# Attention in front of two MoE layers on one core: AV's last 64 keys in half-width products, the mixed step with rotated keys, 1/sum spread on GpSimd and turned a slot later

## The chip, the core and the metric

The kernel runs on one NeuronCore of a Trainium2 chip. The metric is the device time of one launch in microseconds, the median of several executions. TensorE (PE) multiplies, VectorE (DVE), ScalarE (ACT) and GpSimd (POOL) do the element-wise work, SyncE (SP) issues the DMAs. Each engine takes its instructions in the order in which they stand in its own queue.

## What is computed

An attention with a bias that a small network makes from positions, and behind it two MoE-like dense layers on its output, all in float32:

```python
scores = scale * q @ k.T + bias            # bias[h] = relu(log-distance ratio @ w1 + b1) @ w2
attn = exp(scores - max(scores))
attn = attn / (sum(attn) + 1e-9)
x = (attn @ v) as (B*S, H*D)               # B, H, S, D = 4, 8, 576, 64
h = x @ w_in                               # 512 -> 2048 -> 512
x = (h * clip(h + 3, 0, 6) / 6) @ w_out
y = (sigmoid(x @ w_gate) * (x @ w_val)) @ w_out2   # 512 -> 1536 -> 512
```

## The kernel before

The program has four stages. The **bias stage** (lines 508 to 593) makes the position bias in 36 groups G of 16 rows: DVE, and ACT for one tile of every second group, make four hidden tiles (L570, L572), PE multiplies them (L578), ACT evacuates each group in two pieces (L557), and SP writes it to DRAM (`nbias`, L560), from where `load_bias` fetches it. Then comes **attention** (slots of two steps, `slot_of_two`), then the first dense layer (`out1`, `project`), then the second (`gate_val`, `out2`).

Attention treats 16 units n, each a pair of heads of one batch. A unit has nine steps s of 128 query rows: steps 0 to 7 are 128 rows of one head (head s % 2, rows 128 * (s // 2)), and step 8, the mixed step, holds the last 64 rows of both heads, head 0 in partitions 0 to 63 and head 1 in 64 to 127. A slot holds two steps, so a unit is 4.5 slots, and even and odd units lie differently in them.

For a step, `scores` (L342) makes q times k in two halves of 288 keys, with q and k each as a high and a low float32r part; DVE adds the bias and takes the row extreme (L346); ACT takes the exponential with the row sum (`expo`, L362). The probabilities are turned on PE, 128 keys by 128 rows at a time (`trans`, L400), and copied to `ptm`, DVE and ACT in turns. Of 576 keys, 512 go so in four pieces (head 0 the first 512, head 1 the last 512), and the remaining 64 keys of both heads are turned together in one piece into `ptr` (`trans_rem`, L415). In the mixed step, `trans` turns 64 rows of each head apart (L408, eight turns of 64 by 128, one group per head), and `trans_rem` two pieces more (L418, L419); `Pm`, the mixed step's probabilities, has 64 zero columns in front for that.

`av` multiplies: for g = 0 to 3 two products of 64 output columns each, one per head, which fill the two halves of the array (L432), and for the remaining 64 keys one product of 128 columns, whose weights are v of both heads in block form (L435). `AV` sets in which slot each goes. A unit's AV is done in two halves `a` of 288 query rows, each in one slot with g = 0 to 2 and the next one with g = 3 and the remaining keys; behind it `av_out` multiplies by `inv` (L444).

`inv` is 1/sum with queries along the free dimension. `invert` adds 1e-9 to the row sums and takes the reciprocal on DVE (L368, L369), and ACT spreads each sum over 64 or 128 columns of `spread` (L373), one copy after the unit's step 5 and two after step 8. `turn_inv` turns `spread` on PE (L379, three and two turns) into a tile of the ring `tr`, and ACT and DVE copy that to `inv`. The ring `tr` has three tiles in PSUM, for all turns. `invert` is called a slot behind its step, `turn_inv` two slots behind, below scores and AV.

`prep` splits the next unit's q and k into high and low parts, q's high part on ACT (L310), the rest on GpSimd (L314, L318). `load_qk` fetches q and k for that into `early`; for unit 1 it is called in the bias stage at G = 20. Weights for the dense layers are taken in by `load.whole()` at every sixth slot, with work on ACT, DVE and GpSimd (L175 to L193).

The Tile framework lays each engine's queue out by its own estimate of when operands are ready, so the order in a queue is near the order of the code, but not the same.

Of the kernel before, what the change touches and what calls it, by code (L numbers as in the profile page):

```python
# [18 lines left out]
P = 128  # L19
# [77 lines left out]
def block_kernel(ctx: ExitStack, tc: tile.TileContext, q, k, v, mlp, w_in, w_out, w_gate, w_val, w_out2, dist_d,  # L97
# [12 lines left out]
    one = keep.tile([P, 1], F32, name="one")  # L110
    slots = [keep.tile([P, 2, 512], F32R, name=f"slot{i}") for i in range(NPRE)]
# [166 lines left out]
    Pm = [apool.tile([P, S + 64], F32, name=f"pm{i}") for i in range(2)]  # L278
# [18 lines left out]
    def load_bias(p, c):  # L297
        n = min(P, S - P * c)
        rows_of = nbias[c][15 : 15 + n * (8 * RK - 1)].rearrange("(i q) -> i q", i=n)
        for h in range(2):  # L300
            o = bias_t[c][:, h] if c < 4 else bias_m[64 * h : 64 * h + 64]
            nc.sync.dma_start(o, rows_of[:, RK * (2 * p + h) : RK * (2 * p + h) + S])
# [29 lines left out]

    def scores(t):
# [4 lines left out]
        for a in range(2):  # L338
            mm = [(h, c, r) for h, c in todo for r in range(2)]
            for i, (h, c, r) in enumerate(mm):  # L340
                q0 = (0, S + P)[h] + P * c if c < 4 else (512, S)[h]
                last_s[0] = nc.tensor.matmul(ps[:, a, 0:HS], Q[:, q0 : q0 + P], K[:, r, h, HS * a : HS * a + HS],  # L342
                                 start=(i == 0), stop=(i == len(mm) - 1))
# [7 lines left out]
    def probs(t):  # L351
        n, s = seq[t]
        if s < 8:
            c, h = divmod(s, 2)
            if h == 0:
                pts[n, c] = a2.tile([P, 2, S], F32, name="p", bufs=3)
            return pts[n, c][:, h]
        return Pm[n % 2][:, 64:]
# [6 lines left out]
    def invert(n, c0, c1):  # L365

        r = sums[n % 3][:, 2 * c0 : min(2 * c1, NSTEP)]
        nc.vector.tensor_scalar(out=r, in0=r, scalar1=1e-9, scalar2=None, op0=ALU.add)  # L368
        nc.vector.reciprocal(r, r)  # L369
        for s0, s1, w in ((0, 6, 64),) if c1 == 3 else ((6, 8, 64), (8, 9, P)):  # L370
            o = spread[:, 64 * s0 : 64 * s0 + (s1 - s0) * w].rearrange("p (s w) -> p s w", w=w)
            i = sums[n % 3][:, s0:s1].unsqueeze(2).to_broadcast(o.shape)
            nc.scalar.copy(o, i)  # L373
# [20 lines left out]
    def trans(t):  # L394
# [7 lines left out]
        else:  # L402
            pm = Pm[n % 2]
            for h in range(2):
                ps = pp.tile([P, 4, P], F32, name="tr", bufs=3)
                r = slice(64 * h, 64 * h + 64)
                for kc in range(4):
                    nc.tensor.transpose(ps[:, kc, 0:64], pm[r, 64 + 64 * h + P * kc : 64 + 64 * h + P * kc + P],  # L408
                                        ident[r, r])
                evac("AV"[h], ptm[:, h, :, 512:S], ps[:, :, 0:64])  # L410

    def trans_rem(n, c):
# [3 lines left out]
        if c == 3:  # L416
            pm = Pm[n % 2]
            nc.tensor.transpose(ps[:, 1], pm[:, 0:P], ident)  # L418
            nc.tensor.transpose(ps[0:64, 2], pm[:, S : S + 64], ident)  # L419
            evac("A", ptr[0:64, 512:S], ps[0:64, 2, 0:64])  # L420
            evac("V", ptr[64:P, 512:S], ps[64:P, 1, 64:P])
        evac("A", ptr[:, P * c : P * c + P], ps[:, 0])

    def av(n, a, g):
# [9 lines left out]
        else:  # L434
            nc.tensor.matmul(ps[:, 0:HS], vt[:, 8:10].rearrange("p a d -> p (a d)"), ptr[:, cols], start=False, stop=True)  # L435
# [27 lines left out]
    def slot_of_two(i):  # L463

        for t in steps(i):
# [17 lines left out]
        for t in steps(i - 2):  # L483
            n, s = seq[t]
            if s in (5, 8):
                turn_inv(n, s // 6 * 3, s // 6 * 2 + 3)
# [19 lines left out]
    with ExitStack():  # L506
# [11 lines left out]
        nc.vector.memset(one, 1.0)  # L518
        nc.scalar.activation(low[0][:, 0:1], one, AF.Relu)
# [7 lines left out]
        for i in range(2):  # L527
            nc.gpsimd.memset(Pm[i][:, 0:64], 0.0)
# [35 lines left out]
        for G in range(NG):  # L564
# [24 lines left out]
            if G == 20:  # L589
# [336 lines left out]
```

## Time and profile before

| | before |
|---|---|
| median of 3 runs | 1162.75 us (1162.29 to 1164.39) |
| the profiled execution | 1162.39 us |
| its span on the core | 1160.6 us |
| bias stage, attention, first dense layer, second | 0 to 60, 60 to 345, 345 to 743, 743 to 1160 us |

Windows of the trace give the busy time of each engine in a stretch, which shows what a stage has to spare. The waits say what PE stood still for. The timeline of PE gives the start of each run of equal matmuls; since PE works in order, the distance between two starts is what the run between them took, switches of the array included. A float32 product shows as two records per instruction there (`x4` is two instructions), a float32r product or a turn as one. Starts are rounded to 0.01 us.

### The profile page before, as it was taken

To read this page: it belongs to the slowest core of one execution; us is meant where nothing else is said; L and a number is where in the kernel's file an instruction comes from. 1 tells how busy PE (TensorE), PEld (TensorE's weight loads), DVE (VectorE), ACT (ScalarE), POOL (GpSimd) and SP (SyncE) were. 2 spreads that over 40 slices of the span, in tenths; PEclk is the share of its full clock that TensorE was granted. 3 is DMA by queue.
4 is the path that set the end of the run, shared out by engine and by line. 5 is a ranking of instruction groups with operands and counts; after the bars stand their busy time and mean duration, and the time that the engine had idled before them with its cause. 6 is when DMAs were issued, how large, how long until landed. Compare 5 with 4: busy or idle time off the path is not lost.

```text
span 1160.6 us, 19146 instructions
## 1 busy us (share of the span) xinstructions
PE 1139.1 (98%) x6862; PEld 1012.1 (87%) x6862; DVE 776.1 (67%) x1495; ACT 587.6 (51%) x1296; POOL 424.3 (37%) x342
## 2 busy tenths in 40 slices
PE   8799999999999999999999999999999999999998
PEld 3277777777779999999999999999899898998997
DVE  8977887878868887456377685585367655644443
ACT  7888877877855455454455445342333232221221
POOL 0235545545306343232346545261333223311211
PEclk9999999999999999999999999999999999999999
DMA  6853536354213565349566759976878848757532
GB/s 203 276 170 92 178 96 189 94 148 139 79 55 110 196 218 195 118 171 325 183 228 245 253 189 357 394 260 254 314 254 309 305 165 303 282 186 255 190 109 73
DMA packets 83183, 236.82 MB, mean 204 GB/s; under 512 B 9616, under 2 KB 12304, under 8 KB 83088
## 3 DMA queue, kind: packets, MB, share of 16 engines
q1 hardware_dynamic: 83088, 235.60, 58.5%
q8 instruction: 54, 0.88, 0.3%
q14 instruction: 41, 0.34, 0.1%
HBM read 154.15 MB, written 81.41 MB: 203 GB/s over the span
## 4 chain that ended last, share of the span: by engine, by line
PE 84%; DVE 7%; ACT 2%; issue 2%; POOL 1%; DMA 1%; SPq 0%; DVEq 0%; POOLq 0%; ACTq 0%
PE o L673 17%; PE h L807 10%; PE o L807 10%; PE s L342 6%; PE o L862 6%; PE h L862 5%; PE h L612 5%; PE h L610 5%; PE h L611 5%; PE av L432 5%; PE tr L400 4%; PE av L435 1%; DVE z L186 1%; DVE u L346 1%; DVE x L572 1%
## 5 line engine op out<-in xcount | busy, mean ns | idle before, releaser
L673 PE MATMUL o<-gh,slot 128*128 128x384 f32 x768 | 195.1, 334 | 1.8 <-DVE take L392 1.8
L673 PEld LDWEIGHTS o<-gh,slot 128*128 128x128 f32 x768 | 138.5, 188 | 2.4 <-DVE take L392 2.1
L673 PE MATMUL o<-gl,slot 128*128 128x384 f32 x384 | 128.5, 335 | 0.5 <-DVE gl L659 0.5
L362 ACT ACTIVATE p<-u,stat 128x576 f32<-128x576 f32 x128 | 98.7, 774 | 29.2 <-DVE stat L346 28.6
L342 PE MATMUL s<-k,q 128*128 128x288 f32 x640 | 111.1, 309 | 0.3 <-DVE stat L346 0.3
L346 DVE CUSTOM_DVE_ANT_0 u<-s,bias 128x576 f32<-128x576 f32 x128 | 93.5, 752 | 23.9 <-PE s L342 22.8
L843 POOL TENSOR_TENSOR gp<-s,gp 128x384 fp32r<-128x384 f32 x36 | 39.4, 1107 | 177.0 <-ACT gp L842 92.7
L658 ACT CAST gh<-g 128x384 fp32r<-128x384 f32 x94 | 48.2, 513 | 97.7 <-DVE g L617 97.4
L617 DVE SCALAR_TENSOR_TENSOR g<-g,h 128x384 f32<-128x384 f32 x94 | 51.5, 548 | 68.4 <-ACT g L616 68.4
L659 DVE TENSOR_TENSOR gl<-g,gh 128x384 fp32r<-128x384 f32 x94 | 63.2, 672 | 48.5 <-ACT gh L658 47.4
L193 POOL TENSOR_TENSOR hl<-corners,hl 128x512 fp32r<-128x512 f32 x42 | 57.2, 1365 | 93.9 <-ACT hl L192 77.6
L342 PEld LDWEIGHTS s<-k,q 128*128 128x128 f32 x640 | 88.8, 189 | 2.1 <-DVE stat L346 1.0
L616 ACT ACTIVATE g<-h,half 128x384 f32<-128x384 f32 x94 | 54.3, 578 | 52.0 <-PE h L612 51.5
L807 PE MATMUL o<-x,slot 128*128 128x384 f32 x432 | 78.4, 336 | 1.4 <-DVE sum L787 1.4
L432 PE MATMUL av<-ptm,vn 128*64 128x288 f32 x512 | 77.5, 419 | 0.7 <-DVE x L444 0.7
L807 PE MATMUL h<-x,slot 128*128 128x384 f32 x432 | 77.8, 335 | 0.0
L807 PEld LDWEIGHTS o<-x,slot 128*128 128x128 f32 x432 | 75.1, 188 | 2.0 <-DVE sum L787 1.7
L807 PEld LDWEIGHTS h<-x,slot 128*128 128x128 f32 x432 | 75.2, 188 | 0.7
L400 PE MATMUL tr<-ident,p 128*128 128x128 f32 x512 | 72.2, 275 | 2.3 <-ACT inv L390 1.5
L673 PEld LDWEIGHTS o<-gl,slot 128*128 128x128 f32 x384 | 72.1, 188 | 1.2 <-DVE gl L659 1.2
L843 POOL TENSOR_TENSOR x<-s,x 128x384 fp32r<-128x384 f32 x36 | 40.3, 1128 | 84.2 <-ACT x L842 50.2
L314 POOL TENSOR_TENSOR k<-early,one 128x576 fp32r<-128x576 f32 x30 | 35.4, 1202 | 95.1 <-PE s L342 52.9
(157 smaller groups left out, 2734.1 us busy)
## 6 DMA issues: line engine op xcount, KB each, us to landing
w<-hl SPq DMA_DIRECT2D x67, 512.0 KB, 3.4
slot<-w SPq DMA_DIRECT2D x67, 512.0 KB, 5.9
raw<-in_part_dram SPq DMA_DIRECT2D x50, 512.0 KB, 4.0
x<-xc SPq DMA_DIRECT2D x56, 384.0 KB, 6.2
sum<-sum SPq DMA_DIRECT2D x72, 256.0 KB, 3.4
early<-xc SPq DMA_DIRECT2D x28, 384.0 KB, 6.3
nbias<-ptm SPq DMA_DIRECT2D x36, 295.5 KB, 2.7
early<-in_part_dram SPq DMA_DIRECT2D x32, 288.0 KB, 4.3
```

What stands on the lines that cost most here:

```text
L342: last_s[0] = nc.tensor.matmul(ps[:, a, 0:HS], Q[:, q0 : q0 + P], K[:, r, h, HS * a : HS * a + HS], start=(i == 0), stop=(i == len(mm) - 1))
L346: last_u[0] = nc.vector.tensor_tensor_reduce(out=halves(u), in0=ps[:, :, 0:HS], in1=halves(bt), op0=ALU.add, op1=ALU.min, scale=-0.125, sc ...
L362: nc.scalar.activation(probs(t), us.pop(t), AF.Exp, bias=low[n % 2][:, s : s + 1], scale=-1.0, accum_out=sums[n % 3][:, s : s + 1])
L400: nc.tensor.transpose(ps[:, kc], pts[n, c][:, h, 64 * h + P * kc : 64 * h + P * kc + P], ident)
L432: nc.tensor.matmul(ps[64 * h : 64 * h + 64, 0:HS], vt[:, 4 * h + g], ptm[:, h, g, cols], start=(g == 0), stop=False)
L610: nc.tensor.matmul(ps[:, 0:TW], wh, XH[:, c], start=(c == 0), stop=False)
L611: nc.tensor.matmul(ps[:, 0:TW], wl, XH[:, c], start=False, stop=False)
L659: last_g[0] = nc.vector.tensor_tensor(out=gl, in0=g, in1=gh.bitcast(F32), op=ALU.subtract)
L673: nc.tensor.matmul(os[c][:, 0:TW], sl[:, r, P * c : P * c + P], x, start=(first and r == 0 and x is gh), stop=(last and x is gl))
L807: nc.tensor.matmul(ps[b], sl[:, r, o : o + P], x[:, c, s], start=(k < 4 and i == 0), stop=(i == len(mm) - 1), skip_group_check=True)
L843: nc.gpsimd.tensor_tensor(out=G[:, i, 1], in0=s, in1=G[:, i, 0].bitcast(F32), op=ALU.subtract)
L862: nc.tensor.matmul(os[i], x[:, P * i : P * i + P], slots[(base + 14 + e) % NALL][:, r], start=first, stop=last)
```

## The change

- AV's remaining 64 keys are two products of 64 output columns, one per head, instead of one of 128 (`av`).
- In the mixed step, head 1's keys are taken in rotated order: 64 to 575, then 0 to 63. So both heads' first 512 columns of `Pm` are turned together, 4 turns of 128 by 128 and one copy (DVE in even units, ACT in odd), and the remaining 64 columns of both in one turn. The zero columns of `Pm` go. For the order, `scores` makes head 1's second half of that step in pieces of 224 and 64 columns, and `load_bias` fetches its bias rows in two pieces.
- `invert` adds 1e-9 as a tensor (`tiny`), and spreads on GpSimd instead of ACT.
- `turn_inv` is called three slots behind its step, above the slot's scores.
- `load_qk(1)` is called at G = 33.

```diff
@@ load_bias
-            nc.sync.dma_start(o, rows_of[:, RK * (2 * p + h) : RK * (2 * p + h) + S])
+            i = rows_of[:, RK * (2 * p + h) : RK * (2 * p + h) + S]
+            if c == 4 and h == 1:
+                nc.sync.dma_start(o[:, 0:512], i[:, 64:S])
+                nc.sync.dma_start(o[:, 512:S], i[:, 0:64])
+            else:
+                nc.sync.dma_start(o, i)
@@ scores
+    def keys(s, h, a):
+
+        if s < 8 or h == 0:
+            return [(HS * a, 0, HS)]
+        return [(64, 0, HS)] if a == 0 else [(64 + HS, 0, HS - 64), (0, HS - 64, 64)]
...
-            mm = [(h, c, r) for h, c in todo for r in range(2)]
+            mm = [(h, c, r, part) for h, c in todo for r in range(2) for part in keys(s, h, a)]
@@ invert
-        nc.vector.tensor_scalar(out=r, in0=r, scalar1=1e-9, scalar2=None, op0=ALU.add)
+        nc.vector.tensor_tensor(out=r, in0=r, in1=tiny.to_broadcast(r.shape), op=ALU.add)
...
-            nc.scalar.copy(o, i)
+            nc.gpsimd.tensor_tensor(out=o, in0=i, in1=one.unsqueeze(2).to_broadcast(o.shape), op=ALU.mult)
@@ trans
-            pm = Pm[n % 2]
-            for h in range(2):
-                ps = pp.tile([P, 4, P], F32, name="tr", bufs=3)
-                r = slice(64 * h, 64 * h + 64)
-                for kc in range(4):
-                    nc.tensor.transpose(ps[:, kc, 0:64], pm[r, 64 + 64 * h + P * kc : 64 + 64 * h + P * kc + P],
-                                        ident[r, r])
-                evac("AV"[h], ptm[:, h, :, 512:S], ps[:, :, 0:64])
+            ps = pp.tile([P, 4, P], F32, name="tr", bufs=3)
+            for kc in range(4):
+                nc.tensor.transpose(ps[:, kc], Pm[n % 2][:, P * kc : P * kc + P], ident)
+            evac("VA"[n % 2], ptm[:, :, :, 512:S], ps.rearrange("p c (h q) -> p h c q", h=2))
@@ trans_rem
-            pm = Pm[n % 2]
-            nc.tensor.transpose(ps[:, 1], pm[:, 0:P], ident)
-            nc.tensor.transpose(ps[0:64, 2], pm[:, S : S + 64], ident)
-            evac("A", ptr[0:64, 512:S], ps[0:64, 2, 0:64])
-            evac("V", ptr[64:P, 512:S], ps[64:P, 1, 64:P])
+            nc.tensor.transpose(ps[0:64, 1], Pm[n % 2][:, 512:S], ident)
+            for h in range(2):
+                evac("AV"[h], ptr[64 * h : 64 * h + 64, 512:S], ps[0:64, 1, 64 * h : 64 * h + 64])
@@ av
-            nc.tensor.matmul(ps[:, 0:HS], vt[:, 8:10].rearrange("p a d -> p (a d)"), ptr[:, cols], start=False, stop=True)
+            for h in range(2):
+                nc.tensor.matmul(ps[64 * h : 64 * h + 64, 0:HS], vt[:, 8 + h], ptr[:, cols], start=False, stop=True)
@@ slot_of_two
+        for t in steps(i - 3):
+            n, s = seq[t]
+            if s in (5, 8):
+                turn_inv(n, s // 6 * 3, s // 6 * 2 + 3)
         for t in steps(i):
             scores(t)
...
-        for t in steps(i - 2):
-            n, s = seq[t]
-            if s in (5, 8):
-                turn_inv(n, s // 6 * 3, s // 6 * 2 + 3)
@@ the bias stage
-            if G == 20:
+            if G == 33:
                 load_qk(1)
```

How the queues stand now is shown at three places; the line numbers of the changed program are a few higher (L342 is L354 there, L379 is L391, L400 is L412, L415 is L423, L432 is L438).

On PE in unit 5, behind AV's first half (`s` are scores, `tr` turns, `pm` the mixed step's probabilities, `spread` the sums), before:

```order
L379 MATMUL tr<-ident,spread 128x128 x3
L400 MATMUL tr<-ident,p 128x128 x4
L408 MATMUL tr<-ident,pm_233 128x64 x4
L342 MATMUL s<-k_230,q_228 128x288 x4
L408 MATMUL tr<-ident,pm_233 128x64 x4
L342 MATMUL s<-k_230,q_228 128x288
L415 MATMUL tr<-ident,p 128x128
L418 MATMUL tr<-ident,pm_233 128x128
L419 MATMUL tr<-ident,pm_233 64x128
```

and now:

```order
L412 MATMUL tr<-ident,p 128x128 x4
L417 MATMUL tr<-ident,pm_234 128x128 x4
L423 MATMUL tr<-ident,p 128x128
L425 MATMUL tr<-ident,pm_234 64x128
L354 MATMUL s<-k_231,q_229 128x288 x4
L391 MATMUL tr<-ident,spread 128x128 x3
L354 MATMUL s<-k_231,q_229 128x288 x4
```

The half-height turns, which stood in two groups with scores between them (in the eight odd units; in the eight even ones all eight stand together), are four full ones, and the turns of `spread` stand inside the scores.

On PE and on GpSimd around unit 7's second `turn_inv`, PE before:

```order
L435 MATMUL av<-ptr,vn 128x288
L379 MATMUL tr<-ident,spread 128x128 x2
L400 MATMUL tr<-ident,p 128x128 x8
L342 MATMUL s<-k_230,q_228 128x288 x7
L415 MATMUL tr<-ident,p 128x128
L342 MATMUL s<-k_230,q_228 128x288
L432 MATMUL av<-ptm,vn 64x288 x6
```

PE now:

```order
L442 MATMUL av<-ptr,vn 64x288 x2
L412 MATMUL tr<-ident,p 128x128 x8
L423 MATMUL tr<-ident,p 128x128
L354 MATMUL s<-k_231,q_229 128x288 x8
L438 MATMUL av<-ptm,vn 64x288
L391 MATMUL tr<-ident,spread 128x128 x2
L438 MATMUL av<-ptm,vn 64x288 x5
```

and GpSimd now, where `q` and `k` are the next unit's `prep`:

```order
L385 TENSOR_TENSOR spread<-stat,one 128x384
L320 TENSOR_TENSOR k_232<-early,one 128x576
L324 TENSOR_TENSOR k_232<-early,k_232 128x576
L320 TENSOR_TENSOR k_232<-early,one 128x576
L324 TENSOR_TENSOR k_232<-early,k_232 128x576
L324 TENSOR_TENSOR q_230<-early,q_230 64x640
L324 TENSOR_TENSOR q_230<-early,q_230 64x576
L385 TENSOR_TENSOR spread<-stat,one 128x128 x2
```

The turns of `spread` moved behind the scores and into a run of AV products, which they part into one and five; this is so in units 3, 7 and 11. The spread of the second sums stands behind the whole `prep` on GpSimd.

On SP in the bias stage, from group 16 on (`early` of 64x1152 is half of k, `bias` the bias of 128 rows), before:

```order
L560 DMA nbias_80<-ptm 128x591 x4
L291 DMA early<-in_part_dram 64x1152 x2
L560 DMA nbias_80<-ptm 128x591 x4
L560 DMA nbias_81<-ptm 128x591 x2
L302 DMA bias_224<-nbias_79 128x576 x2
L560 DMA nbias_81<-ptm 128x591 x6
L560 DMA nbias_82<-ptm 128x591 x4
```

and now:

```order
L566 DMA nbias_81<-ptm 128x591 x5
L308 DMA bias_225<-nbias_80 128x576
L566 DMA nbias_81<-ptm 128x591 x3
L308 DMA bias_225<-nbias_80 128x576
L566 DMA nbias_82<-ptm 128x591 x2
L292 DMA early<-in_part_dram 64x1152
L566 DMA nbias_82<-ptm 128x591 x4
L292 DMA early<-in_part_dram 64x1152
L566 DMA nbias_82<-ptm 128x591 x2
L566 DMA nbias_83<-ptm 128x591 x4
```

Both halves of k stood behind the write of group 19; now one stands behind that of group 25 and one behind that of group 29.

## Rows read from the trace of the kernel before

**Rows 1.** Windows: length, busy us of PE, PEld, DVE, ACT, POOL, clock.

```profile
60.00:345.00 285.00, 281.71 (x2063) 215.52 (x2062) 222.69 (x574) 226.75 (x591) 128.83 (x98) 1.00 0.41 121
345.00:743.00 398.00, 395.55 (x2276) 393.97 (x2275) 269.37 (x426) 195.92 (x380) 167.91 (x132) 1.00 0.62 223
```

**Rows 2.** Waits of PE in attention: us in total, times, longest.

```profile
PE tr L400 <- ACT inv L390: 1.5, 3, 0.5
PE tr L400 <- DVE ptm L392: 0.7, 3, 0.2
```

**Rows 3.** Timeline of PE in unit 6: start us, us.

```profile
171.13 0.71 PE L432 MATMUL av<-ptm,vn 128*64 128x288 f32 x4
171.77 0.75 PE L435 MATMUL av<-ptr,vn 128*128 128x288 f32 x2
172.36 1.04 PE L400 MATMUL tr<-ident,p 128*128 128x128 f32 x8
173.23 0.27 PE L415 MATMUL tr<-ident,p 128*128 128x128 f32 x1
...
175.03 1.68 PE L432 MATMUL av<-ptm,vn 128*64 128x288 f32 x12
176.64 0.55 PE L379 MATMUL tr<-ident,spread 128*128 128x128 f32 x3
177.02 1.04 PE L400 MATMUL tr<-ident,p 128*128 128x128 f32 x8
...
179.67 0.75 PE L435 MATMUL av<-ptr,vn 128*128 128x288 f32 x2
180.36 0.47 PE L408 MATMUL tr<-ident,pm 64*128 64x64 f32 x8
180.76 0.33 PE L415 MATMUL tr<-ident,p 128*128 128x128 f32 x1
180.93 0.27 PE L418 MATMUL tr<-ident,pm 128*128 128x128 f32 x1
```

**Rows 4.** Timeline of PE in unit 5, the mixed step's turns.

```profile
160.65 0.60 PE L400 MATMUL tr<-ident,p 128*128 128x128 f32 x4
161.18 0.46 PE L408 MATMUL tr<-ident,pm 64*128 64x64 f32 x4
...
162.93 0.27 PE L415 MATMUL tr<-ident,p 128*128 128x128 f32 x1
```

**Rows 5.** Windows of DVE's line 572 in the bias stage: length, busy us.

```profile
45.00:50.45 5.45, 5.42 (x5) 1.00 0.98 315
50.45:54.40 3.95, 3.95 (x11) 1.00 0.50 192
```

**Rows 6.** Timeline of GpSimd in the bias stage.

```profile
43.34 3.88 POOL L314 TENSOR_TENSOR k<-early,one 128x576 fp32r<-128x576 f32 x2 [41.90 <-DMA early<-in_part_dram]
47.18 3.08 POOL L318 TENSOR_TENSOR k<-early,k 128x576 fp32r<-128x576 f32 x2
```

**Rows 7.** Timeline of ACT in the bias stage.

```profile
51.61 1.09 ACT L557 ACTIVATE ptm<-s,corr,early 128x112 f32<-128x112 f32 x2 [2.51 <-PE s L578]
```

**Rows 8.** Window of all engines in the bias stage, as in rows 1.

```profile
50.30:61.50 11.20, 10.61 (x90) 4.81 (x90) 9.22 (x23) 9.16 (x18) 1.55 (x1) 1.00 0.53 201
```

**Rows 9.** SP's queue in the bias stage: start of the first, time to the last.

```profile
37.42 2.20 SPq L291 DMA_DIRECT2D early<-in_part_dram  x2
...
46.58 15.27 SPq L560 DMA_DIRECT2D nbias<-ptm  x10
```

**Rows 10.** Timeline of GpSimd in unit 7's `prep`.

```profile
190.56 2.25 POOL L314 TENSOR_TENSOR k<-early,one 128x576 fp32r<-128x576 f32 x2 [8.18 <-PE s L342]
...
199.42 1.42 POOL L318 TENSOR_TENSOR q<-early,q 64x576 fp32r<-64x576 f32 x1 [2.21 <-ACT q L310]
```

**Rows 11.** Timeline of PE at the same place.

```profile
201.81 1.68 PE L432 MATMUL av<-ptm,vn 128*64 128x288 f32 x12 [0.23 <-DVE x L444]
```

**Rows 12.** One line of DVE: times, ns min/median/max, first and last start.

```profile
L659 DVE TENSOR_TENSOR gl<-g,gh x94: 545/559/1644, 358.0 to 737.9; 128x384 fp32r<-128x384 f32 x94
```

More of the change, by code (lines that the diff above doesn't have):

```diff
@@ L110, in block_kernel @@
     one = keep.tile([P, 1], F32, name="one")
+    tiny = keep.tile([P, 1], F32, name="tiny")
     slots = [keep.tile([P, 2, 512], F32R, name=f"slot{i}") for i in range(NPRE)]
@@ L277, in block_kernel @@
     Ks = [apool.tile([P, 2, 2, S], F32R, name=f"k{i}") for i in range(2)]
-    Pm = [apool.tile([P, S + 64], F32, name=f"pm{i}") for i in range(2)]
+    Pm = [apool.tile([P, S], F32, name=f"pm{i}") for i in range(2)]
     ident = apool.tile([P, P], F32, name="ident")
@@ L338, in scores @@
         for a in range(2):
-            mm = [(h, c, r) for h, c in todo for r in range(2)]
-            for i, (h, c, r) in enumerate(mm):
+            mm = [(h, c, r, part) for h, c in todo for r in range(2) for part in keys(s, h, a)]
+            for i, (h, c, r, (k0, o, w)) in enumerate(mm):
                 q0 = (0, S + P)[h] + P * c if c < 4 else (512, S)[h]
-                last_s[0] = nc.tensor.matmul(ps[:, a, 0:HS], Q[:, q0 : q0 + P], K[:, r, h, HS * a : HS * a + HS],
-                                 start=(i == 0), stop=(i == len(mm) - 1))
+                last_s[0] = nc.tensor.matmul(ps[:, a, o : o + w], Q[:, q0 : q0 + P], K[:, r, h, k0 : k0 + w],
+                                             start=(i == 0), stop=(i == len(mm) - 1))
         u = a2.tile([P, S], F32, name="u", bufs=3)
@@ L357, in probs @@
             return pts[n, c][:, h]
-        return Pm[n % 2][:, 64:]
+        return Pm[n % 2]
     def expo(t):
@@ L518, in block_kernel @@
         nc.vector.memset(one, 1.0)
+        nc.vector.memset(tiny, 1e-9)
         nc.scalar.activation(low[0][:, 0:1], one, AF.Relu)
@@ L526, in block_kernel @@
         make_identity(nc, ident)
-        for i in range(2):
-            nc.gpsimd.memset(Pm[i][:, 0:64], 0.0)
         nc.vector.tensor_scalar(out=tbl, in0=tbl, scalar1=w1c, scalar2=None, op0=ALU.mult)
```

## The prediction, made before the changed kernel was run

> **What bounds the kernel now.** I read the windows of the stages first. In attention PE is busy 281.71 of 285.00 us, in the first dense layer 395.55 of 398.00, at the full clock (granted clock 1.00, its 2.4 GHz level), while DVE, ACT and GpSimd have a fifth or more to spare in attention [rows 1]. So in attention and behind it the time is PE's, and an edit is worth what it takes out of PE's queue; the dense layers keep their work and shift as a whole. PE's rows there can overlap, and so I take costs from distances between starts in its timeline [rows 3, 4]. Its waits come second: 3.3 us of idle time in attention (285.00 less 281.71), of which two kinds concern the turns' ring [rows 2]. The bias stage is of another sort: there PE waits for DVE and ACT, and the rows to look at are DVE's line 572, GpSimd and ACT [rows 5 to 8].
>
> **PE's work in attention, part by part.** A turn of 128 by 128 takes 0.109 us: eight take 172.36 to 173.23. Of AV, a pair of 64-column products takes 0.64 us alone (171.13 to 171.77) and three pairs 1.61 (175.03 to 176.64), so one pair more in a run is (1.61 - 0.64) / 2 = 0.485 us, and a run has 0.155 us of entering and leaving on top. The 128-column product takes 0.59 (171.77 to 172.36) [rows 3].
>
> - *AV's last keys.* A pair of 0.485 takes the place of 0.59. But the first turn behind a pair is longer: three turns take 0.38 there (176.64 to 177.02) and not 0.33. That leaves 0.055 us, in 32 places: **-1.8 us**. It supposes that two products that read the same columns of `ptr` go side by side as pairs with different columns do.
> - *The mixed step's turns, odd units.* From 160.65 to 162.93 PE makes four full turns, both groups of half-height turns and five scores: 2.28 us [rows 4]. Four turns are 0.44; a score is 0.14 (173.23 to 175.03 holds one turn and twelve scores, 1.80 us [rows 3]), five are 0.70. The half-height turns with their four switches of the array cost 1.14 us, four full turns 0.44: 0.70 us in eight units, **-5.6 us**.
> - *The same, even units.* Eight together take 0.40 (180.36 to 180.76), the AV product ahead of them 0.10 more than elsewhere (0.69, 179.67 to 180.36), the turn behind them 0.17 and not 0.11: 0.56 against 0.44, in eight units **-1.0 us** [rows 3].
> - *One turn less* for the remaining 64 columns, 16 times 0.109: **-1.7 us**.
> - *Scores in pieces.* 32 products of 288 columns become 224 and 64. No row has a float32r product of 64 columns. From below it costs only a second start: a score takes 0.133 to 0.14 us for 288 columns, which at 2.4 GHz are 0.12, so at least 0.013. From above it is no longer than a turn, which loads 128 columns of weights as well, 0.109, less the 0.027 of its own 64 columns: 0.082. Eight half-height turns, each with a load of 128 columns, take 0.40, that is 0.05 each [rows 3]; those can go two at a time, so I put a load and a start at some 0.06 and take 0.035 (0.06 less 0.027): **+1.1 us** (0.4 to 2.6).
> - *Turns of 1/sum.* Inside scores they cost what they cost before. In units 3, 7 and 11 they part a run of six AV products into one and five, as the queue shows: four pairs' time instead of three (0.485), a second entering and leaving (0.155), a second long turn (0.05) and a slower score ahead of it (about 0.1), 0.8 us each: **+2.4 us**.
>
> Together -1.8 - 5.6 - 1.0 - 1.7 + 1.1 + 2.4 = **-6.6 us** (-7.3 to -5.1 with the ends for the pieces).
>
> On the pieces, the rows show turns that follow each other in 0.05 us, each with a load of its own [rows 3]. The Trainium skill, *TensorE: Matmul & The Clock Gate*, section "LDWEIGHTS (loading the stationary operand)", gives a load as its columns divided by 1.2 GHz, whatever its rows, so 0.107 us for 128. By that a 64-column product would be held up to 0.107 and the pieces would cost 2.6 us, 1.5 more; the half-height rows speak against it, unless loads into two halves of the array run at once.
>
> **The bias stage.** `load_qk(1)` moves, and with it GpSimd's `prep` of unit 1, which ran from 43.34 to 50.3, as soon as k had landed [rows 6]. In just that time four of DVE's hidden tiles (480 columns wide) took 5.4 us; the ones behind them, wider still, take 0.38 each (3.95 us for 11, the outer ones in part) [rows 5]. So DVE lost 5.4 - 1.5 = 3.9 us, and ACT stood 2.51 us behind PE for it [rows 7]. Behind that ACT has little room: it is busy 9.16 of 11.20 us, and most of the rest is the end of this same wait [rows 8]. What comes back is the smaller: **-2.5 us**. From above it is 3.9. From below it is 0, where GpSimd's work falls on the last hidden tiles instead. Now k's second half stands behind the write of group 29, the fourth of ten that took 15.27 us from 46.58 on: at 46.6 + 4 x 1.5 - 2.5 = 50.2. k took 5.9 us to land (37.42 to 43.34), so GpSimd begins at about 56, when the stage, 2.5 us shorter, has its last write at 61.9 - 2.5 = 59.4 [rows 6, 9]. At most the last group's tiles meet it. Unit 1's scores come behind those of unit 0, 40 products of 0.14 and some 36 turns of 0.109, which is 9.5 us more, beginning at about 57.7 (60.2, near where the window of attention begins, less 2.5); `prep`, 7 us from 56 on, is ready at 63.
>
> **Waits of PE.** In each of three places 0.2 us on DVE's copy of a turned tile: there the mixed step filled two tiles of the ring of three, now one, so I take these off: **-0.7 us**. The three on ACT's copy of `inv`, 1.5 us [rows 2], I leave: ACT has less to do but DVE, which it follows, hardly. Ends: all 3.3 us gone, or as much more as the first rival says.
>
> **Costed at nothing.** The spread on GpSimd: 384 columns are 384/576 of 1.13 us, 0.75, and two of 128 0.3 each, 1.35 us a unit (from two copies in 2.25 [rows 10]); GpSimd is busy 128.83 of 285 us [rows 1], and `turn_inv` comes a slot later; the cover gone is the third rival. ACT loses three copies a unit and DVE half a copy on average, both beside PE. The add with `tiny` reads two tensors in SBUF; DVE's line 659, of that form, takes 559 ns in the median and 1644 at most [rows 12], so a stretched add stays possible and I credit nothing. SP's extra piece of bias (64 columns, 64 rows, four times) lies ahead of a step eight steps later.
>
> **The sum.** 6.6 + 2.5 + 0.7 = 9.8 us off the profiled execution's 1162.39: 1152.6. The median of the runs shown lies 0.4 us above that execution: **1153.0 us**.
>
> **The rivals.**
>
> 1. *The queues of DVE and ACT give half of it back.* Both are busy 78 to 80% of attention [rows 1], in a queue's order, and where weights are taken in they are late already: PE's waits on turns stand there [rows 2]. If PE comes earlier it waits longer. For it: those waits; against it: ACT's spreads go. Half of 6.6 lost, and the 0.7: 1157.0. Chance 0.18.
> 2. *The bias stage gives nothing,* since GpSimd's four operations fall on the last hidden tiles: 1155.5. Chance 0.10.
> 3. *The spread comes late (slower).* PE waits in order at the turn of `spread`, with scores and AV behind it. GpSimd has the second spread behind the whole `prep`. In unit 7 that ends at 199.42 + 1.42 = 200.84 [rows 10]; with 0.6 the spread is there at 201.4. PE reaches it one pair behind the entry at 201.81 [rows 11], of which 0.23 was a wait: near 202.1. So 0.7 us are left there and more elsewhere. If GpSimd is late by two of its operations of 1.4 us in every unit, 2.1 of 2.8 us are left as a wait in unit 7's kind, and I put 1.4 in the mean. It decides from 9.8 us / 16 = 0.6 us a unit on; at 1.4 us in all 16 units the time is 1153.0 + 22.4 = 1175. Chance 0.04.
> 4. *The pairs don't go side by side (slower).* Two products that stream the same columns of `ptr` might go one after the other, as no pair of before does it: 0.485 us more in 32 places, 15.5 us: 1168.5. Against it: each half of the array has its own stream in the pairs of before. Chance 0.05.
> 5. *More than I count:* 3.9 us in the bias stage and all waits of PE gone: 1149.0. Chance 0.05.
>
> **How the numbers follow.** The forecast has 0.58, with its own range of 1150.5 to 1155.5 (pieces 0.4 to 2.6, waits of 1.5 more or less). The range of 1149.5 to 1157.5 takes in rival 2, most of 1 and half of 5, and leaves out both slower cases. A measurement of this kernel can tell about 0.2%, 2.3 us: faster means below 1160.4. The forecast and rivals 1, 2 and 5 hold 0.91, of which 0.04 may still end above that: faster 0.87, same 0.05, slower 0.08.
>
> **What would show it.** In the profile after: no DVE row of line 572's kind above 0.6 us before GpSimd's first operation, PE's first scores 2.5 us earlier than before; L442's two instructions (four records) within 0.5 us of the pair ahead of them; 0.44 us for the four turns of `pm`; scores of 224 and 64 together 0.17; attention some 7 us shorter than 285, and the dense layers as long as before. Waits of PE at the turn of `spread` with GpSimd as releaser would be rival 3, records of L442 that start 0.24 us apart instead of in pairs rival 4. A dense layer that has grown longer would make the whole argument wrong, that time taken from attention goes through to the end.

## The result, and the profile after

The changed kernel takes **1176.49 us** (median of 4 runs, 1175.67 to 1178.09), against 1162.52 before on the same chip: ratio 1.0117, interval 1.0104 to 1.0130. It is slower by 14 us; 1153.0 was forecast. The profiled execution's span is 1173.7 us (before: 1160.6).

The windows of the profile after (length, then busy us of PE, PEld, DVE, ACT, POOL) answer rows 1:

```profile
60.00:345.00 285.00, 267.10 (x1996) 202.87 (x1994) 229.15 (x549) 204.72 (x517) 156.17 (x145) 1.00 0.42 118
345.00:743.00 398.00, 395.12 (x2277) 390.87 (x2277) 271.90 (x430) 197.38 (x385) 170.57 (x133) 1.00 0.60 213
```

In attention PE now stands idle for 17.9 us, not 3.3. PE's waits there (us in total, times, longest) answer rows 2:

```profile
PE tr L391 <- ACT ptm L402: 10.3, 14, 1.6
PE tr L423 <- ACT ptr L402: 4.9, 6, 1.1
PE s L354 <- DVE stat L358: 1.6, 3, 0.5
PE av L438 <- DVE ptm L404: 0.5, 3, 0.2
```

All are waits on ACT's and DVE's handling of other tiles: the largest stands at the turn of `spread` (L391), but it ends when ACT has copied an earlier turned tile out of the ring. None is on GpSimd's `spread`. From the start of the first score to the start of the last AV product, attention takes 297.4 us (before 283.8). PE's own work did become cheaper. The timeline of PE after, unit 6, answers rows 3:

```profile
172.94 0.71 PE L438 MATMUL av<-ptm,vn 128*64 128x288 f32 x4
173.47 0.66 PE L442 MATMUL av<-ptr,vn 128*64 128x288 f32 x4
174.06 1.09 PE L412 MATMUL tr<-ident,p 128*128 128x128 f32 x8
174.99 0.27 PE L423 MATMUL tr<-ident,p 128*128 128x128 f32 x1
175.02 2.01 PE L354 MATMUL s<-k,q 128*128 128x288 f32 x14
176.96 1.68 PE L438 MATMUL av<-ptm,vn 128*64 128x288 f32 x12
```

Two pairs of AV with entering and leaving take 1.12 us (172.94 to 174.06), where a pair and the 128-column product took 1.23; the eight turns behind take 0.93 instead of 0.87. The turn at 174.99 and twelve scores, two of them in pieces (14 records), take 1.97 us, where [rows 3] have 1.80 for whole ones: 0.085 for each score in pieces. The mixed step's four turns take 0.44 us (unit 5):

```profile
160.99 0.60 PE L417 MATMUL tr<-ident,pm 128*128 128x128 f32 x4
161.43 0.27 PE L423 MATMUL tr<-ident,p 128*128 128x128 f32 x1
```

The bias stage: GpSimd's `prep` of unit 1, the windows of DVE's hidden tiles (L578, which was L572; length, busy us), and PE's first scores after and before. They answer rows 5 and 6:

```profile
54.57 2.44 POOL L320 TENSOR_TENSOR k<-early,one 128x576 fp32r<-128x576 f32 x2 [53.27 <-DVE x L578]
45.00:50.45 5.45, 5.45 (x15) 1.00 0.94 326
50.45:54.40 3.95, 3.95 (x11) 1.00 0.94 295
56.53 1.32 PE L354 MATMUL s<-k,q 128*128 128x288 f32 x8 [0.41 <-ACT ptm L563]
60.26 1.33 PE L342 MATMUL s<-k,q 128*128 128x288 f32 x8
```

DVE makes fifteen tiles in the 5.45 us in which it made five (tiles cut by an end of the window counted), and scores begin 3.73 us earlier. So attention begins 3.7 us ahead, ends 10 us behind, and the dense layers add 3.

Where attention loses is seen at an intake of weights. The timelines of DVE, GpSimd, ACT and PE after, unit 8 (start, us, line, idle time before and what ended it):

```profile
233.21 0.75 DVE L358 CUSTOM_DVE_ANT_0 u<-s,bias 128x576 f32<-128x576 f32 x1
236.15 1.41 DVE L177 TENSOR_SCALAR z<-z 128x512 f32<-128x512 f32 x1 [1.76 <-ACT z L176]
237.59 1.52 DVE L185 TENSOR_SCALAR z<-z 128x512 int32<-128x512 int32 x1
239.03 0.74 DVE L358 CUSTOM_DVE_ANT_0 u<-s,bias 128x576 f32<-128x576 f32 x1
```

```profile
234.23 1.42 POOL L324 TENSOR_TENSOR k<-early,k 128x576 fp32r<-128x576 f32 x1
235.73 3.10 POOL L324 TENSOR_TENSOR q<-early,q 64x640 fp32r<-64x640 f32 x2
```

```profile
233.92 0.78 ACT L374 ACTIVATE p<-u,stat 128x576 f32<-128x576 f32 x1
234.69 0.77 ACT L374 ACTIVATE p<-u,stat 128x576 f32<-128x576 f32 x1
235.45 0.66 ACT L176 ACTIVATE z<-raw 128x512 f32<-128x512 f32 x1
239.88 0.78 ACT L374 ACTIVATE p<-u,stat 128x576 f32<-128x576 f32 x1 [2.12 <-DVE stat L358]
```

```profile
240.95 0.33 PE L423 MATMUL tr<-ident,p 128*128 128x128 f32 x1 [1.04 <-ACT ptr L402]
```

DVE stands at a weight operation for 1.76 us, because ACT makes its operand behind two exponentials. Then both weight operations take 1.4 to 1.5 us beside GpSimd's `prep`, and the next `u` starts at 239.03, 5.1 us after the last one ended. ACT runs dry, then PE. Over attention DVE's wait for ACT at that line is (us in total, times, longest):

```profile
DVE z L177 <- ACT z L176: 14.5, 7, 2.9
```

### The profile page after: what moved, and what is told of

It reads as the page before. It is cut to its first block, busy times and chain, and to the rows that moved or that the text cites. A ratio compares the mean times of both kernels' runs of the same rounds, so it can differ in the third digit from the quotient of the medians.

```text
span 1173.7 us, 19270 instructions
## 1 busy us (share of the span) xinstructions
PE 1136.9 (97%) x6878; PEld 1011.0 (86%) x6878; DVE 786.2 (67%) x1488; ACT 573.3 (49%) x1240; POOL 452.3 (39%) x388
## 4 chain that ended last, share of the span: by engine, by line
PE 80%; DVE 5%; ACT 4%; issue 3%; POOL 2%; DMA 2%; SPq 0%; POOLq 0%; DVEq 0%; ACTq 0%
PE o L679 16%; PE h L813 11%; PE o L813 10%; PE o L868 6%; PE h L868 6%; PE h L616 5%; PE h L617 5%; PE h L618 5%; PE av L438 4%; PE s L354 4%; PE tr L412 3%; ACT p L374 2%; DVE z L177 1%; PE av L442 1%; DVE u L358 1%
## 5 line engine op out<-in xcount | busy, mean ns | idle before, releaser
L354 PE MATMUL s<-k,q 128*128 128x288 f32 (+2 forms) x672 | 110.1, 304 | 2.4 <-DVE stat L358 2.0
L354 PEld LDWEIGHTS s<-k,q 128*128 128x128 f32 x672 | 91.8, 190 | 4.1 <-DVE stat L358 3.1
L438 PE MATMUL av<-ptm,vn 128*64 128x288 f32 x512 | 78.5, 419 | 0.9 <-DVE ptm L404 0.5
L412 PEld LDWEIGHTS tr<-ident,p 128*128 128x128 f32 x512 | 56.0, 141 | 23.7 <-issue 15.8
L412 PE MATMUL tr<-ident,p 128*128 128x128 f32 x512 | 74.0, 279 | 0.1
```

The lines of the kernel that those rows point to most:

```text
L354: last_s[0] = nc.tensor.matmul(ps[:, a, o : o + w], Q[:, q0 : q0 + P], K[:, r, h, k0 : k0 + w], start=(i == 0), stop=(i == len(mm) - 1))
L412: nc.tensor.transpose(ps[:, kc], pts[n, c][:, h, 64 * h + P * kc : 64 * h + P * kc + P], ident)
L438: nc.tensor.matmul(ps[64 * h : 64 * h + 64, 0:HS], vt[:, 4 * h + g], ptm[:, h, g, cols], start=(g == 0), stop=False)
```

## The experiments

Three suspects stood at this point: the address of tiles (the new tile `tiny` moves all that is allocated behind it by 32 bytes a partition), the place of the turns of 1/sum, and the spread on GpSimd.

**a_align**: the change, with `tiny` as a second column of the tile `one`, so that nothing moves.

```diff
-    one = keep.tile([P, 1], F32, name="one")
-    tiny = keep.tile([P, 1], F32, name="tiny")
+    one2 = keep.tile([P, 2], F32, name="one")
+    one, tiny = one2[:, 0:1], one2[:, 1:2]
```

> The changed kernel, but `tiny` is the second column of the tile that holds `one`, so that the weight slots lie where they lay before the change (in the changed kernel all that is allocated behind `tiny` lies 32 bytes per partition further). Theory of the address: products of the second dense layer that stream x, 177 ns apart after the change, are 173 ns apart again, and the time falls by about 3 us to 1173.5. Rival, that the longer second layer comes from the later start or other traffic: 177 ns and 1176.5 stay.

1172.09 us, 4.4 less. **b_pad**: before, with a tile of one column set aside there.

```diff
+    pad = keep.tile([P, 1], F32, name="pad")
```

> The kernel before with one more tile of 32 bytes per partition allocated behind `one` and set once, nothing else. Theory of the address: the products of the second dense layer that stream x go from 173 to 177 ns apart, and the time rises by about 3 us, to 1165.5. Rival: no change, 1162.5.

1166.42, 4.0 more than before. PE's products of the second dense layer that stream `x`, in before, after, a_align and b_pad (count, busy us, mean ns):

```profile
L807 PE MATMUL h<-x,slot 128*128 128x384 f32 x424 | 76.4, 335 | 0.0
L813 PE MATMUL h<-x,slot 128*128 128x384 f32 x432 | 79.3, 340 | 0.0
L813 PE MATMUL h<-x,slot 128*128 128x384 f32 x432 | 77.8, 335 | 0.0
L809 PE MATMUL h<-x,slot 128*128 128x384 f32 x422 | 77.5, 340 | 0.0
```

The two kernels with moved tiles have 340 ns, the other two 335. The address is worth 4.0 to 4.4 us of the loss; the other 10 us have another cause.

**a_turn**: a_align with `turn_inv` back, two slots behind and below scores and AV. **a_act**: the change with the spread back on ACT, and the add as before (of each edit only the main lines are shown).

```diff
@@ a_turn
-        for t in steps(i - 3):
+        for t in steps(i - 2):
@@ a_act
-            nc.gpsimd.tensor_tensor(out=o, in0=i, in1=one.unsqueeze(2).to_broadcast(o.shape), op=ALU.mult)
+            nc.scalar.copy(o, i)
```

> The changed kernel with slots as before, and `turn_inv` back two slots behind its step, below scores and AV; the spread stays on GpSimd. Theory of the turn (PE stands, with scores behind it, at the turn of 1/sum for a tile of the ring of three that ACT frees late): waits of PE in attention fall from 18 us to under 5, time about 1158. Theory of GpSimd (the spread makes GpSimd's run longer, DVE's weight operations beside it are stretched, u is late, and all else follows): waits stay at 13 us or more, time 1170 or more.

> The changed kernel with the spread back on ACT and the one-tensor add (no `tiny`, so slots as before); `turn_inv` stays three slots behind and above scores. Theory of the turn: PE still stands at the turn of 1/sum, time 1168 to 1173. Theory of GpSimd: waits under 5 us, DVE's weight operations near the 0.6 to 0.7 us of before, time about 1158.

a_turn takes 1171.27, within a us of a_align: with the spread on GpSimd, the turn's place is not it. a_act takes **1154.42** (ratio 0.9928, 0.9913 to 0.9943), 17.7 us less than a_align and faster than before. The loss goes when the spread and the add are taken back together.

**a_both**: both edits. It was to show that the late turn does not matter either way.

> The changed kernel with both taken back: `turn_inv` two slots behind and below scores, spread on ACT, no `tiny`. What is left is AV in half-width products, the rotated mixed step and `load_qk(1)` at G = 33. Both theories: waits of PE in attention about 3 us as before, the bias stage 3.7 us shorter, attention about 6 us shorter: 1153 to 1156. If it is over 1160, the cause is in the three parts that are left.

1163.17, 8.75 above a_act: a miss, kept for the end of this section. Then the parts alone, each put into before. **b_qk**: `load_qk(1)` at G = 33. **b_av**: the halves in `av`. **b_rot**: the rotated mixed step (`trans`, `trans_rem`, `scores` and `load_bias`; of its edit one line is shown). **b_late**: `turn_inv` three slots behind, above scores.

```diff
@@ b_qk
-            if G == 20:
+            if G == 33:
@@ b_av
+            for h in range(2):
+                nc.tensor.matmul(ps[64 * h : 64 * h + 64, 0:HS], vt[:, 8 + h], ptr[:, cols], start=False, stop=True)
@@ b_rot
+            evac("VA"[n % 2], ptm[:, :, :, 512:S], ps.rearrange("p c (h q) -> p h c q", h=2))
@@ b_late
-        for t in steps(i - 2):
+        for t in steps(i - 3):
```

> The kernel before with `load_qk(1)` at G = 33 alone. Theory (four of DVE's hidden tiles waited for GpSimd's `prep`): PE's first scores come 3.7 us earlier, as in the changed kernel, and the time falls by 3 to 3.7 us, to 1159. Rival (the later `prep` delays unit 1, so that it is given back in attention): 1161 to 1163.

> The kernel before with AV's last 64 keys in two 64-column products alone. By the prediction's sum -1.8 us: 1160.8; if the queues of DVE and ACT take it back, 1162.5.

> The kernel before with the mixed step's rotated keys alone (four full turns, scores in pieces of 224 and 64, `Pm` without zero columns). By the prediction's sum -5.6 - 1.0 - 1.7 + 1.1 = -7.2 us: 1155.4. With the pieces at what the changed kernel's trace shows (0.088 us each, 2.8 us): 1157.0. If the queues take half back: 1159 to 1160.

> before with turn_inv three slots behind its step and above the slot's scores, the spread on ACT, and nothing else of the change. With the rotated step the late turn was worth 8 to 9 us (a_act against a_both: 1154.42 and 1163.17), and the rotated step without it cost 5.3 us (b_rot). If the two belong together (the rotated step brings PE sooner to the turn of the sums, which then holds a tile of the turns' ring), the late turn alone gives at most the waits that PE had there before: 1160.5 to 1163. If the late turn is worth its gain by itself: 1153 to 1157.

b_qk 1158.25 (-4.2), b_av 1161.18 (-1.3; 0.9976 to 0.9993), b_late 1161.31 (-0.9; 0.9978 to 0.9998), and b_rot 1167.79: **+5.3** where 5.5 to 7.2 of gain were expected.

Now the spread. **c_dummy**: a_act, with GpSimd making the same three spreads again into a tile that nobody reads. **c_relief**: a_align with k's high parts in `prep` on ACT. **c_phase**: a_align with the intake of weights a slot later.

```diff
@@ c_dummy
             nc.scalar.copy(o, i)
+            o = aside[:, 64 * s0 : 64 * s0 + (s1 - s0) * w].rearrange("p (s w) -> p s w", w=w)
+            nc.gpsimd.tensor_tensor(out=o, in0=i, in1=one.unsqueeze(2).to_broadcast(o.shape), op=ALU.mult)
@@ c_relief
-PREP_ON = "APPP"
+PREP_ON = "AAPP"
@@ c_phase
-            if i % EVERY == 0 and i > 10 and load.n < NPRE:
+            if i % EVERY == 1 and i > 10 and load.n < NPRE:
```

> a_act (the change with the spread of 1/sum back on ACT, 1154.42 us) with the same three spreads made a second time by GpSimd, into a tile that nobody reads. Nothing waits for GpSimd's copies, and PE, DVE and ACT have their work in the order of a_act; GpSimd gets the busy time that the change gave it (some 27 us more in attention). Theory A (GpSimd's longer and later run lies beside DVE's weight operations and stretches them, and u, the exponentials and PE come behind): most of the 17.7 us between a_align and a_act come back, 1164 to 1172, mean of DVE's two one-tensor weight operations above 900 ns. Theory B (the cost is in the way of the sums themselves: the spread arrives late, or DVE's queue is laid out otherwise): 1154 to 1156, as a_act.

> a_align (the change with the aligned tile, 1172.09 us) with the high parts of k in prep on ACT instead of GpSimd. The spread stays on GpSimd, which has 1.13 us twice a unit less, some 36 us in attention, so its busy time there is near that of before (129 us); ACT has some 21 us more. Theory A (GpSimd's busy time beside DVE's weight operations): DVE's one-tensor weight operations below 750 ns in the mean, time 1154 to 1161. Theory B (the spread through GpSimd): 1169 to 1174, as a_align.

> a_align with the intake of weights one slot later in its cycle of six slots. GpSimd's work and the way of the sums are the same; the weight operations on DVE meet other parts of GpSimd's run. Theory A: the time follows the stretch: by about what DVE's four weight operations lose or gain in sum against a_align (there some 20 us above their free length), so between 1155 and 1173, not above. Theory B: 1170 to 1174 whatever the stretch is.

c_dummy takes 1154.91, as a_act. The windows of attention of a_act and c_dummy (columns as in rows 1):

```profile
60.00:345.00 285.00, 280.27 (x2093) 216.52 (x2092) 228.55 (x569) 225.82 (x585) 134.38 (x102) 1.00 0.41 122
60.00:345.00 285.00, 280.28 (x2095) 217.02 (x2094) 227.51 (x569) 225.81 (x585) 161.05 (x150) 1.00 0.42 122
```

GpSimd is busy 26.7 us longer, and PE loses nothing. So GpSimd's busy time by itself, with the other queues in a_act's order, costs nothing. It does not stretch DVE's two one-tensor weight operations there either: they take 724 and 479 ns in the mean, and 1238 and 1453 in a_align. What c_dummy leaves open is a stretch in a_align's order. c_relief (1157.46) came out as theory A said, but its queue orders differ too; c_phase (1183.61) is above what either theory allowed.

**d_read**: c_dummy with PE turning GpSimd's copy. **d_order** and **d_best**: a_align and a_act with the whole intake released by the slot's last `u`.

```diff
@@ d_read
-            nc.tensor.transpose(ps[:, c % 3], spread[:, P * c : P * c + P], ident)
+            nc.tensor.transpose(ps[:, c % 3], aside[:, P * c : P * c + P], ident)
@@ d_order, d_best
-                with tc.issue_after(last_v[0].ins):
+                with tc.issue_after(last_u[0].ins):
```

> c_dummy (1154.91 us) with one operand changed: PE's turns take GpSimd's copy of the sums instead of ACT's, which is made and read by nobody. All five queues have the order of c_dummy. c_dummy showed that GpSimd's busy time alone costs nothing, so two theories are left. Theory B (the sums arrive late by way of GpSimd, PE waits at their turn or behind it): 1160 to 1172, with GpSimd as releaser of waits at the turn of the sums. Theory C (the way by GpSimd costs nothing; the scheduler lays DVE's queue out otherwise when ACT has no spread to do, and puts the two one-tensor weight operations ahead of two steps' u, beside GpSimd's prep): 1154 to 1156.

> a_align (1172.09 us) with the weights' intake released by the last u of the slot instead of by the load of v: DVE's one-tensor weight operations stand behind two steps' u, where a_align has them ahead. The spread stays on GpSimd, ACT has no spread. Theory C (order of DVE's queue): 1154 to 1162, with DVE's waits on ACT's z gone (12.2 us in a_align). Theory B (the sums late by way of GpSimd): 1168 to 1173.

> a_act (1154.42 us) with the weights' intake released by the last u, as in d_order. Theory C: the order in a_act is good already, so 1152 to 1156; it is the version of the two orders with the spread on ACT. Theory B says nothing of it: 1154 to 1155.

d_read takes 1157.02: the way of the sums by GpSimd costs 2.1 us at most, hardly clear of noise, and not 17. d_order (1168.0) can't be read, since d_best (1165.49) shows that this edit costs a_act 11 us: it also holds back the weights' DMA, and puts all four weight operations in a row. DVE around the same intake in d_read:

```profile
228.93 0.76 DVE L358 CUSTOM_DVE_ANT_0 u<-s,bias 128x576 f32<-128x576 f32 x1
229.61 0.67 DVE L176 TENSOR_SCALAR z<-z 128x512 f32<-128x512 f32 x1
230.20 0.51 DVE L453 TENSOR_TENSOR x<-av,inv 128x192 f32<-128x192 f32 x2
230.63 0.68 DVE L406 COPY ptm<-tr 128x512 f32<-128x512 f32 x1
231.23 0.41 DVE L184 TENSOR_SCALAR z<-z 128x512 int32<-128x512 int32 x1
```

These two weight operations stand two `u` later in DVE's queue than in the changed kernel, wait for nothing, and are apart. Is that place the cause? Comparing the starts of DVE's rows of `u` step by step, a_align falls behind d_read at the ten intakes alone, and by nothing between. **e_place** is a_align with DMA and work released apart, so that in seven of the ten intakes DVE's weight operations stand where a_act has them (but for one operation in the last of the seven); the three middle ones (steps 38, 74, 110) stay. `all_u` holds the instructions that make `u`, in order.

```diff
-            for stage in (self.dma, self.magnitude, self.assemble):
-                stage(i)
-            self.finish(i, nc.gpsimd)
+            with tc.issue_after(last_v[0].ins):
+                self.dma(i)
+            with tc.issue_after(all_u[-self.back].ins):
+                self.magnitude(i)
+                self.assemble(i)
+                self.finish(i, nc.gpsimd)
@@
+                load.back = (3, 3, 5)[i // EVERY % 3]
```

> a_align (1172.09 us) with the weights' DMA released as there, and the work on them held back behind the u of five steps ago, or of three, so that DVE's four weight operations stand where a_act has them in seven of ten intakes (one or two u later than in a_align), and as in a_align in the three intakes of the middle phase (around steps 38, 74 and 110). GpSimd makes the spread, ACT has none. a_align loses its 15 us against d_read in ten jumps of 1.7 to 2.2 us, each at an intake, and nothing between. Theory C (place in DVE's queue): the jumps go in the seven intakes and stay, some 1.8 us each, in the three: 1159 to 1163. Theory D (that ACT has no spread to do, or the sums' way by GpSimd, whatever the place): the jumps stay in all: 1169 to 1173.

1159.92. The places are the numbers of `u` ahead of DVE's four weight operations in the first, middle and third intake; the losses are us against d_read, from step 18 to step 135:

| | first | middle | third | lost in the seven | in the three middle |
|---|---|---|---|---|---|
| d_read | 22 22 24 24 | 39 40 40 40 | 48 50 50 50 | 0 | 0 |
| a_align | 20 20 22 24 | 38 38 39 40 | 46 46 48 50 | 9.3 | 5.6 |
| e_place | 22 22 24 24 | 38 38 39 40 | 48 50 50 50 | -1.1 | 5.6 |
| a_both | 22 24 24 24 | 38 38 38 38 | 48 50 50 51 | -0.8 | 7.4 |
| f_both | 22 24 24 24 | 39 40 41 42 | 48 50 50 51 | -0.8 | 2.6 |
| f_act | 22 22 24 24 | 40 40 41 41 | 48 50 50 50 | -0.9 | -1.0 |
| c_relief | 22 22 24 24 | 39 40 40 40 | 46 46 50 50 | 2.1 | -0.8 |

DVE's timeline in e_place, first an intake that was left (step 74), then one that was moved:

```profile
193.25 1.43 DVE L177 TENSOR_SCALAR z<-z 128x512 f32<-128x512 f32 x1 [1.75 <-ACT z L176]
194.71 1.52 DVE L185 TENSOR_SCALAR z<-z 128x512 int32<-128x512 int32 x1
196.15 0.74 DVE L361 CUSTOM_DVE_ANT_0 u<-s,bias 128x576 f32<-128x576 f32 x1
...
232.24 1.30 DVE L177 TENSOR_SCALAR z<-z 128x512 f32<-128x512 f32 x1
233.46 0.51 DVE L455 TENSOR_TENSOR x<-av,inv 128x192 f32<-128x192 f32 x2
233.89 0.67 DVE L408 COPY ptm<-tr 128x512 f32<-128x512 f32 x1
234.49 0.41 DVE L185 TENSOR_SCALAR z<-z 128x512 int32<-128x512 int32 x1
```

The loss goes where the place was changed, and stays where it was not. ACT makes `z` behind the same exponential in d_read, a_align and e_place; a few instructions of PE and ACT near the intakes stand up to three places elsewhere in e_place than in a_align. The first operation is stretched in both places; behind two `u` that costs nothing. How much of the loss at the early place is DVE's wait for ACT, and how much the stretch, is not shown. c_relief fits: its weight operations stand as in d_read but for the third intake. So does c_phase, whose trace falls behind d_read's at the intakes: 4.3, 4.5 and 2.9 us at those that it brought to steps 28, 64 and 100.

The table holds a_both's miss as well: its whole loss lies at the three middle intakes, where all four weight operations stand ahead of step 38's `u`. **f_both** is a_both with these three worked on a slot later, **f_act** is a_act with the same.

```diff
+            if i % 18 == 0 and i > 10 and load.n < NPRE:
+                load.first()
+            elif i % 18 == 1 and i > 10 and load.n < NPRE:
+                load.second(all_u[-2])
```

Here `first` issues the DMA, and `second` does the work behind the first `u` of the slot.

> a_both (the rotated step and the halves of AV with the turns of the sums two slots behind and the spread on ACT, 1163.17 us) with the three middle intakes of weights (around steps 38, 74 and 110) worked on a slot later: DVE's four weight operations stand behind the u of steps 39 to 42 there, one each, where a_both has all four ahead of step 38's. Against d_read, a_both loses 6.6 us in three jumps of 2 to 2.4 us, at these three intakes alone. If the place in DVE's queue makes them, and the turns' own place nothing: the jumps go, 1155.5 to 1158.5. If the turns of the sums two slots behind cost by themselves with the rotated step (PE's waits on ACT's copy of inv, 6.4 us): 1161 to 1164.5.

> a_act (1154.42 us) with the same later work at the middle intakes, where it has DVE's weight operations behind the u of steps 39 and 40 already. Both theories: 1153 to 1156; below 1153 only if the one u of step 39 that stands behind a weight operation in a_act still costs something.

f_both takes 1157.43: of the 8.75 us between a_both and a_act, 5.7 are the place of the intake. The other 3 may be the turn's place, for PE's waits on `inv` are still there; three of the four, 4.9 us, stand at the middle intakes, where f_both still loses 2.6 (PE's waits, f_both):

```profile
PE tr L434 <- ACT inv L413: 5.3, 4, 1.9
```

f_act is the fastest, **1153.27** (0.9919, 0.9905 to 0.9934). It has no such waits, and is 4.2 us shorter than f_both: with the rotated step the later turn pays, where alone it gave 0.9 (b_late).

## Why the prediction was wrong

- **The step that failed** is "Costed at nothing": the spread on GpSimd, and with it ACT's lost copies. I named GpSimd's free time and the later turn as cover, and that cover held (c_dummy 0.5 us, d_read some 2 more). What I left out is that the change moves instructions that it does not name. With no spread on ACT, the order of DVE's queue puts the weight operations one or two `u` earlier, where DVE waits for ACT and then beside GpSimd. d_read against a_align is 15.1 us, 9.3 at seven intakes and 5.6 at the three middle ones; that the place makes it is shown for the seven, by e_place, and is likely for the three. That the lost copies make the order is not shown apart: a_align also differs from d_read in the add. The changed order could be read in DVE's queue beforehand; the prediction went by those of PE, GpSimd and SP.
- **Rival 1** had the right place, the queues of DVE and ACT where weights are taken in, but it let them give back no more than half of 6.6 us and counted ACT's lost spreads as a help.
- **Rival 3** was near in size (1175) for another reason: it had PE wait at the turn of `spread` for GpSimd. No such row is among PE's waits after; the wait is DVE's on ACT, at L177, 14.5 us in seven places.
- **"The dense layers keep their work and shift as a whole"** failed, by 4.4 us, for the 32 bytes of `tiny`. The prediction gave a longer dense layer as the sign that would break it, and had no price for it. The add with `tiny`, credited with nothing, had nothing to give: 338 and 626 ns after, 162 and 627 before (L380 and L368, six and three columns).
- **The mixed step.** Its four turns take 0.44 us, as forecast; the pieces were mis-sized, 32 x 0.085 = 2.7 us and not 1.1, just above the end of 2.6. That is the dearer end, where a load of 128 columns behind a 64-column product is not hidden. The half-height turns that spoke against it start in pairs, one of each head, 0.01 us apart, and the pairs some 0.06: they do go two at a time. The Trainium skill, *TensorE: Matmul & The Clock Gate*, section "LDWEIGHTS (loading the stationary operand)", gives a load as its columns divided by 1.2 GHz. By that I had worked out an estimate of 2.6 us for the pieces, and the trace agrees with it (2.7) against my reading.
- **The rotated step was no local edit.** I summed its turns as if nothing else moved; b_rot's +5.3 has the work of the middle intakes ahead of step 38's `u`, as a_both has, and falls 6.9 us behind the kernel before at these three.
- **Turns of 1/sum:** where they part a run of AV products they cost about what was forecast (unit 7 after: 2.63 us for three pairs and two turns, some 0.75 more than [rows 3] give for them unparted). What the later turn brings with the rotated step, 4.2 us (f_both, f_act), was not in the sum.
- **AV's last keys** were right: -1.3 measured, -1.8 forecast; the pairs on the same columns go side by side, so rival 4 falls. In b_av alone the gain is near the noise.
- **The bias stage** was right in mechanism and too small: -4.2 (b_qk) for 2.5; scores come 3.73 us earlier, and rival 2 falls. The step that failed is "what comes back is the smaller": ACT had the room, and about the whole of DVE's 3.9 came back. GpSimd began at 54.57 (forecast about 56), and met the last hidden tiles for 0.3 us at most.
- **Waits of PE:** -0.7 forecast, 14.6 us more came, mostly by the first point.

The way from after to the forecast, by runs: 1176.49, the address -4.4, seven intakes -12.2 (e_place; 10.4 of it at the intakes themselves), and f_act's 1153.27 with the spread on ACT and all ten in place. That this is the forecast's 1153.0 is chance in part. Attention from the first score to the end of the last AV product, in before and in f_act (columns as in rows 1):

```profile
60.26:344.49 284.23, 280.94 (x2059) 214.90 (x2058) 222.21 (x572) 226.12 (x589) 128.10 (x97) 1.00 0.41 121
56.67:336.95 280.28, 275.84 (x2073) 212.81 (x2073) 223.06 (x564) 224.08 (x581) 133.94 (x100) 1.00 0.42 123
```

It is 3.9 us shorter, where 7.3 were forecast: the pieces are dearer by 1.6, and PE stands idle for 4.4 us, 1.8 more than the forecast left. Scores begin 3.6 us earlier and not 2.5, and what lies behind attention is 1.4 us shorter, where nothing was forecast; why is not shown. f_act's later work at the middle intakes is not part of the change; a_act, without it, takes 1154.42.

## What to carry to other kernels

Where a scheduler lays out the queues, read the new order of every engine at every place where a second stream of work (here weights) joins the main one, and not only where the edit is; an edit that only takes work off engines with time to spare can move another engine's instructions. In an in-order queue, side work belongs behind the operation that feeds the critical engine; at the intakes shown here its own stretch was then free. A new tile of one column moves all that lies behind it, which here cost 4 us; as a column of an existing tile it cost nothing.

## What the runs showed of the hardware

- Products of the second dense layer that stream `x` take 340 instead of 335 ns in the mean, and start 177 instead of 173 ns apart, when all that is allocated behind `one`, the weights among it, lies 32 bytes a partition further (b_pad against before, after against a_align). `x` is allocated ahead of `one` and stays where it was. Products that stream `early`, `odd` or `late`, which are allocated behind it and move with the weights, start 173 ns apart (the median) in all four. The program takes 4.0 us more in b_pad, and 4.4 more in after than in a_align. What it is in the addresses is not shown.
- A one-tensor operation of DVE in SBUF that takes 0.41 us alone took up to 1.65 beside GpSimd (L185: 0.41 and 1.52 in e_place, 1.65 at step 46's intake in a_align and after). In the intake shown of after it ends when GpSimd's work has just ended: GpSimd's pair of 3.10 us from 235.73 ends at 238.83, L185 at 239.11. By these rows the price is up to 1.2 us an operation; at e_place's moved intakes, where L177 took up to 1.33, PE felt none of it. The Trainium skill, *GPSIMD Engine Reference*, section "8. Key points", says that the two engines share SBUF interfaces and contend where DVE runs in a two-port mode or reads two SBUF tensors. The stretch agrees with that if these operations run in a two-port mode, which no row here shows.
